# Six first products of the Mish layer inside the retention steps, two second products behind it, the first k in PSUM banks of its own, the second group of q a step sooner

## The chip, the core and the metric

The kernel runs on one core of one Trainium2 chip. The metric is the device time of one execution in microseconds (us). The engines named below are PE (TensorE), DVE (VectorE), ACT (ScalarE), POOL (GpSimd) and SP (SyncE, which here only issues transfers). Each engine takes its own instructions strictly in the order in which they stand in the program.

## What is computed

```python
# q, k, v: (4, 8, 576, 64); x: (2304, 512) tokens
scores = (q @ k^T) / sqrt(64)
ret = scores * Dmat              # Dmat[h] = gamma_h ** (i - j) for i >= j, else 0
x = (ret @ v)                    # (4, 8, 576, 64) -> (2304, 512)
h = x @ w_in                     # (2304, 512) @ (512, 2048)
x = (h * tanh(softplus(h))) @ w_out          # Mish; (2048, 512)
g = x @ w_gate; val = x @ w_val              # (512, 1536) each
out = (silu(g) * val) @ w_out2               # (1536, 512)
```

All in float32. PE multiplies each wide product as three products of two-part operands (a rounded part and the rest of it), so every weight and every activation is first split into such a pair.

## The kernel before

**Retention.** 20 steps `t`: 4 batches, each in 4 chunks of 128 positions and a last one of 64. In a step PE computes the scores of the chunk (`s`, line 505), transposes the next chunk's k and a part of a later q (`turn`, line 436, out to `kT` and `qT` by ACT, a few by DVE), then the product with the running state (`o`, line 575), the new state (`state`, line 549) and the masked scores times v (`o`, line 585), for which DVE must have masked the scores (`p`, line 515). DVE then scales `o` into the tokens `x` (line 598). All transposes go through one PSUM tile with the tag `tt`, so a `turn` waits until the one before it has been copied out.

**Weights.** `w_in` and `w_out` come as 32 pieces of 512 KB, in the order of the list `todo`: in0 to in4, out0, in5, out1, and so on to in15, out11, and then out12 to out15. Counted from 0, in5 is piece 6 and out12 is piece 28. A piece is fetched into one of four buffers `raw`, and takes five instructions of DVE and ACT in two or three passes: ACT scales one half (line 114) and DVE shifts the other (line 115); DVE puts the sign in (line 119) and joins the halves (line 123); ACT casts the first part of the result (line 133), and DVE (in retention POOL) subtracts it to get the second (line 134, `u<-raw,u`). Only then is the piece ready for PE and its buffer is free for the piece four places later. In retention one such pass, with one fetch, stands at the end of each step that is not in `REST`.

**Slots.** The Mish layer runs on blocks of 384 tokens, the first two blocks as 32 slots `s` (16 of each block). The first product of a slot is `g1(s)` (`h`, line 682, 12 matmuls on piece in`s`), its Mish, cast and rest are made by ACT and DVE (lines 733, 740, 744), and the second product `g2(s)` (`acc`, line 716, 12 matmuls on piece out`s`) comes four slots later. `EARLY` is the list of retention steps that hold a first product each: between the transposes and the state products of that step. After retention, `slot(s)` writes `g1(s)`, `g2(s - 4)`, then the Mish of slot `s`, and behind it the passes over further weight pieces: as many as are needed until `2 * s` pieces are done, and then one or two more. `plain1(i)` sends three finished weight quarters back to memory, for the third and later blocks, which use a Strassen scheme (lines 904 and 1298). Everything behind the slots is the same program before and after.

The rows call the weight pieces' buffers `raw`, the finished pieces `u`, and the transposed q and k `qT` and `kT`.

Of the kernel before, what the change touches and what calls it, by code (L numbers as in the profile page):

```python
# [7 lines left out]
F32 = mybir.dt.float32  # L8
# [9 lines left out]
def retention_mish_swiglu(  # L18
# [17 lines left out]
    nc = tc.nc  # L36
    B, H, S, D = q.shape
    NT, DM = out.shape
    F1 = w1_in.shape[1] // 128
    F2 = w2_gate.shape[1] // 128  # L40
    KT = DM // 128
    NP = H // 2
# [3 lines left out]
    LAG = 4  # L46
# [3 lines left out]
    W = (12, 3, 3)  # L50
    NC = 2
    RATES, AHEAD = (2.9, 3.3, 0.4, 1.28, 0.9, 1.0), 45
    EARLY = (9, 11, 14, 17)
    REST = (9, 14, 18, 19)

    xp = ctx.enter_context(tc.tile_pool(name="xp", bufs=1))
    cr = ExitStack()
# [325 lines left out]
    def retention(g1, mish, g_hi, g_lo):  # L383
        with ExitStack() as c0:
# [39 lines left out]

            def turn(name, *items):
                items = [x for x in items if x]
                if not items:
                    return  # L430
                p = ps1.tile([128, 2, 2, NP, 64], F32, tag="tt", name=f"t{name}")
                for z, (n, src, _) in enumerate(items):
                    for pr in range(NP):
                        for r in range(-(-n // 64)):
                            own = slice(64 * r, min(64 * r + 64, n))
                            nc.tensor.transpose(p[:, r, z, pr, :own.stop - own.start], src(pr)[own], ident[own, own])
                for z, (_, _, empty) in enumerate(items):
                    empty(p[:, :, z])

            def q_item(b, g, e, eng=nc.scalar.copy):  # L440
                if b >= B:
                    return None
                x = qkv["q", b, g]
                if g == nsc // 2:
                    n = S - 256 * g
                    qT[b, g] = at.tile([128, NP, n], F32, tag="qTl", name=f"qT{b}_{g}", bufs=1)
                    return (
                        n, lambda pr: x[:, 2 * pr:2 * pr + 2, :],
                        lambda p: nc.scalar.copy(out=qT[b, g], in_=p[:, 0, :, :n]),
                    )  # L450

                def empty(p):
                    if e == 0:
                        qT[b, g] = at.tile([128, NP, 256], F32, tag="qT", name=f"qT{b}_{g}")
                    for r in range(2):
                        (nc.vector.tensor_copy if (b, g, r) == (0, 1, 1) else eng)(
                            out=qT[b, g].rearrange("p a (h n r) -> p h a n r", r=2, h=2)[64 * e:64 * e + 64, :, :, :, r],
                            in_=p[64 * r:64 * r + 64],
                        )

                return 128, lambda pr: x[:, 2 * pr + e, :, :], empty

            def k_item(t):
                if t >= len(steps):
                    return None
                b, sc, n = steps[t]
                src = qkv["k", t]

                def empty(p):
                    kT[t] = at.tile([128, NP, 128], F32, tag="kT", name=f"kT{t}")  # L470
                    if n <= 64:
                        nc.scalar.copy(out=kT[t][:, :, :n], in_=p[:, 0, :, :n])
                    else:
                        nc.scalar.copy(out=kT[t].rearrange("p a (h n) -> p h a n", h=2), in_=p)

                return n, lambda pr: src[:, 2 * pr:2 * pr + 2, :], empty
# [5 lines left out]

            def q_next(t):
                b, sc, n = steps[t]
                due = (b, 1, sc) if sc < 2 else (b, 2, 0) if sc == 2 else (b + 1, 0, sc - 3)
                return q_item(*due) if b or sc > 1 else None

            def scale_v(t):
                if t >= len(steps):
# [42 lines left out]
            due = []  # L532
# [7 lines left out]
            def state(t):  # L540
                b, sc, n = steps[t]
                if sc == nsc - 1:
                    return
                if sc == 0:
                    stp[b] = ps1.tile([128, NP, D], F32, tag="st", name=f"state{b}")
                for pr in range(NP):
                    for e in range(2):
                        h = 2 * pr + e
                        nc.tensor.matmul(
                            stp[b][64 * e:64 * e + 64, pr, :],  # L550
                            lhsT=qkv["k", t][:n, h, :],
                            rhs=vs[t][:n, h, :],
                            start=(sc == 0 and pr == 0),
                            stop=(sc == nsc - 2),
                            skip_group_check=True,
                        )
# [11 lines left out]
            def output(t):  # L568
                b, sc, n = steps[t]
                o = ps1.tile([128, NP, 128], F32, tag="o", name=f"o{t}")  # L570
                if sc:
                    for pr in range(NP):
                        for e in range(2):
                            own = slice(64 * e, 64 * e + 64)
                            nc.tensor.matmul(  # L575
                                o[own, pr, :n], lhsT=sbd[:, pr, own], rhs=q_cols(t)[:, pr],
                                start=(pr == 0), stop=False, skip_group_check=True,
                            )
                state(t)
                if t == 1:  # L580
                    turn("q0_1", q_item(0, 1, 0), q_item(0, 1, 1))
                state_out(t)
                for pr in range(NP):
                    for e in range(2):
                        nc.tensor.matmul(  # L585
                            o[64 * e:64 * e + 64, pr, :n],
                            lhsT=vs[t][:n, 2 * pr + e, :],
                            rhs=pp[t][:n, e, pr, :n],
                            start=(sc == 0 and pr == 0), stop=True, skip_group_check=True,
                        )  # L590
                t0 = b * S + sc * 128
                done = 0
                while done < n:
                    j, off = divmod(t0 + done, T)
                    m = min(n - done, T - off)
                    if j not in xt:
                        new_x(xt, j, "x")
                    nc.vector.tensor_tensor(
                        out=xt[j][:, :, off:off + m],
                        in0=o[:, :, done:done + m],  # L600
                        in1=gout[:, :, sc * 128 + done:sc * 128 + done + m],
                        op=ALU.mult,
                    )
                    done += m
                    if j < 2 and off + m == T:
                        due.extend((j, kk) for kk in range(KT if j == 0 else XS - KT))
# [25 lines left out]
            warm(W[0])  # L632
            turn("q0_0", q_item(0, 0, 0), q_item(0, 0, 1, nc.vector.tensor_copy))
            warm(W[1])
            turn("k0", k_item(0))
            scale_v(0)
            warm(W[2])
            for t in range(len(steps)):
# [36 lines left out]
    with tc.manual_schedule():  # L675
# [70 lines left out]
        def slot(s):  # L746
            b, i = divmod(s, F1)
            if i == 0 and s:
                g2(s - LAG)
            g1(s)  # L750
            if s >= LAG and i:
                g2(s - LAG)
            d, nm, j = xt, "x", b + 1
            parts = () if b + 1 == NC else (i - F1 + 4,) if b and F1 - 4 <= i < F1 - 2 else range(2, KT) if i == F1 - 1 else ()
            mish(s)
            for kk in parts:
                split_hi(d, nm, j, kk)
            g_hi(s)
            g_lo(s)
            for kk in parts:  # L760
                split_lo(d, nm, j, kk, nc.vector)
            if s < F1 + OFF:
                while stage[3] < min(2 * s, n1):
                    run(weights(n1))
            if s >= LAG:
                g2_out(s - LAG)
            if s < F1 + OFF and not parts:
                for _ in range(1 + s % 2):
                    run(weights(n1, True))
            if s == len(EARLY):  # L770
                plain1(0)
            if s % 2 and s > len(EARLY) and s // 2 - 1 < F1 // 2:
                plain1(s // 2 - 1)
            if stage[3] >= n1:
                (third if third.ahead else second)(RATES[s >= F1 + OFF])
            if s == F1 + OFF:
                second(0.0)
# [293 lines left out]
                    second(RATES[3])  # L1071

        FIN1 = (6, 8, 8, 8, 6, 6, 6)
        for s in range(len(EARLY), NS):
            slot(s)
            if s == NS - F1 + 2:
                ya, yb = ysteps("e0", xt[NC], xt[NC + 1])
                ahead += ya + yb[0] + yb[1]
            if s > NS - F1 + 2:
                pop(ahead, 1 + s % 2)  # L1080
            if s >= NS - F1 + 10:
                stream1(s - (NS - F1 + 10))
# [329 lines left out]
```

## Time and profile before

| | |
|---|---|
| median of 3 runs | 892.86 us (890.14 to 893.03) |
| the profiled execution | 894.11 us, of which 892.3 us between its first and its last instruction |
| PE busy in that span | 871.9 us (98%) |
| DVE busy | 652.9 us (73%) |
| ACT busy | 426.6 us (48%) |
| POOL busy | 53.1 us (6%) |

The span is the stretch that the trace covers; times in the rows below are counted from its start. Retention takes it up to 106.4 us, the slots from there to about 225 us. Busy shares are means over stages with different limits, and they don't say which engine another one waits for.

### The profile page before, as it was taken

What the parts mean: (1) busy time and instruction counts of PE and PEld (TensorE: products, weight loads), DVE (VectorE), ACT (ScalarE), POOL (GpSimd) and SP (SyncE); (2) the same over time, 40 slices, a digit from 0 to 9 for tenths busy, and PEclk for the clock granted to TensorE, in tenths of its full rate; (3) what the DMA queues carried; (4) which work ended last, traced back from release to release, by engine and by line L of the source; (5) the groups of instructions that cost most, each with busy time, mean ns of one, the idle gap of its engine ahead of it and who ended that gap; (6) DMA issues with size and microseconds to landing.
All of it is one profiled execution on the core that took longest, in us unless ns stands there. A gap on an engine that the chain in (4) does not pass through costs nothing.

```text
span 892.3 us, 16688 instructions
## 1 busy us (share of the span) xinstructions
PE 871.9 (98%) x6330; PEld 842.0 (94%) x6330; DVE 652.9 (73%) x1271; ACT 426.6 (48%) x835; POOL 53.1 (6%) x47
## 2 busy tenths in 40 slices
PE   7888999999999999999999999999999999999998
PEld 7777899999999999999999999999999999999998
DVE  3886788998777786777786878876676776575772
ACT  3776566645656556565664424263212263222260
POOL 3654300000000000000000000000000000000000
PEclk9999999999999999999999999999999999999999
DMA  9999578577899985799978698978877878877773
GB/s 210 253 231 250 155 209 263 177 236 252 303 325 315 338 285 165 235 335 342 320 269 280 214 335 310 306 245 274 295 251 244 250 252 270 291 256 252 251 246 119
DMA packets 161600, 232.21 MB, mean 260 GB/s; under 512 B 48240, under 2 KB 124272, under 8 KB 161520
## 3 DMA queue, kind: packets, MB, share of 16 engines
q1 hardware_dynamic: 159984, 229.94, 81.4%
q10 hardware_dynamic: 1536, 1.21, 0.5%
q8 instruction: 50, 0.82, 0.4%
q14 instruction: 30, 0.25, 0.1%
HBM read 178.68 MB, written 52.43 MB: 259 GB/s over the span
## 4 chain that ended last, share of the span: by engine, by line
PE 85%; DVE 5%; DMA 5%; ACT 3%; issue 1%; POOL 1%; SPq 0%; ACTq 0%; POOLq 0%; DVEq 0%
PE t L904 29%; PE T L1298 15%; PE te L904 12%; PE e0a L975 7%; PE e1a L975 6%; PE h L682 5%; PE acc L716 4%; DMA raw<-in_moe_w_out_dram 3%; PE s L505 1%; DMA raw<-in_moe_w_in_dram 1%; PE o L585 1%; PE acc L950 1%; DMA v<-in_v_dram 1%; PE idle L630 1%; PE o L575 1%
## 5 line engine op out<-in xcount | busy, mean ns | idle before, releaser
L904 PE MATMUL t<-y,su 128*128 128x384 f32 x1512 | 267.6, 337 | 0.7 <-DVE u L911 0.4
L904 PEld LDWEIGHTS t<-y,su 128*128 128x128 f32 x1512 | 263.8, 188 | 2.9 <-DVE u L911 0.7
L904 PE MATMUL te<-ye,eu 128*128 128x384 f32 x672 | 136.1, 337 | 0.5 <-DVE scratch L911 0.5
L1298 PE MATMUL T<-su,g 128*128 128x256 f32 x1134 | 135.7, 282 | 0.0
L1298 PEld LDWEIGHTS T<-su,g 128*128 128x128 f32 x1134 | 135.6, 190 | 0.0
L904 PEld LDWEIGHTS te<-ye,eu 128*128 128x128 f32 x672 | 113.5, 188 | 5.0 <-DVE scratch L911 0.7
L975 PE MATMUL e1a<-ge,u 128*128 128x512 f32 (+1 forms) x384 | 76.2, 337 | 0.0
L975 PE MATMUL e0a<-ge,u 128*128 128x512 f32 (+1 forms) x384 | 76.1, 337 | 0.0
L682 PE MATMUL h<-xs,u 128*128 128x384 f32 x384 | 72.2, 337 | 0.0
L975 PEld LDWEIGHTS e1a<-ge,u 128*128 128x128 f32 x384 | 61.9, 188 | 6.0
L975 PEld LDWEIGHTS e0a<-ge,u 128*128 128x128 f32 x384 | 62.0, 188 | 5.8
L682 PEld LDWEIGHTS h<-xs,u 128*128 128x128 f32 x384 | 66.8, 188 | 0.3
L716 PE MATMUL acc<-g,u 128*128 128x384 f32 x336 | 63.4, 337 | 1.5 <-DVE u L134 0.9
L716 PEld LDWEIGHTS acc<-g,u 128*128 128x128 f32 x336 | 58.6, 188 | 2.4 <-DVE u L134 1.5
L1167 ACT ACTIVATE sg<-sg 128x384 f32<-128x384 f32 x54 | 28.4, 525 | 58.5 <-DVE sg L911 58.5
L1196 ACT COPY p<-t 128x384 f32<-128x384 f32 x35 | 16.5, 473 | 80.7 <-PE t L904 80.7
L1130 ACT CAST g<-ga 128x384 fp32r<-128x384 f32 x72 | 32.5, 514 | 43.2 <-DVE ga L1175 32.4
L911 DVE TENSOR_TENSOR u<-t,p 128x384 f32<-128x384 f32 x36 | 20.1, 557 | 40.3 <-PE t L904 40.2
L914 DVE TENSOR_TENSOR g<-ga,g 128x384 fp32r<-128x384 f32 x72 | 36.2, 553 | 6.4 <-ACT g L1130 6.2
L911 DVE TENSOR_TENSOR scratch<-te,scratch 128x384 f32<-128x384 f32 x48 | 26.7, 555 | 13.0 <-PE te L904 10.3
L911 DVE TENSOR_TENSOR v<-t,p 128x384 f32<-128x384 f32 x36 | 20.1, 557 | 17.0 <-PE t L904 16.9
L114 ACT ACTIVATE raw<-raw 128x512 f32<-128x512 f32 x32 | 22.1, 692 | 17.7 <-DMA raw<-in_moe_w_out_dram 12.5
(169 smaller groups left out, 1199.5 us busy)
## 6 DMA issues: line engine op xcount, KB each, us to landing
su<-comb SPq DMA_DIRECT2D x126, 512.0 KB, 4.3
su<-fcomb SPq DMA_DIRECT2D x63, 512.0 KB, 4.2
eu<-ecomb SPq DMA_DIRECT2D x56, 512.0 KB, 5.5
comb<-c SPq DMA_DIRECT2D x48, 256.0 KB, 4.8
raw<-in_moe_w_in_dram SPq DMA_DIRECT2D x16, 512.0 KB, 5.8
raw<-in_moe_w_out_dram SPq DMA_DIRECT2D x16, 512.0 KB, 5.4
ecomb<-e SPq DMA_DIRECT2D x32, 256.0 KB, 2.8
ecomb<-u SPq DMA_DIRECT2D x24, 256.0 KB, 4.6
```

The lines of the kernel that those rows point to most:

```text
L114: nc.scalar.activation(hi.bitcast(F32), hi.bitcast(F32), AF.Copy, scale=2.0 ** -112)
L505: nc.tensor.matmul(s[:n, e, pr, :n], lhsT=kT[t][64 * e:64 * e + 64, pr, :n], rhs=q_cols(t)[64 * e:64 * e + 64, pr], start=True, stop=True,)
L682: nc.tensor.matmul(ps, lhsT=u[:, a, kk * 128:(kk + 1) * 128], rhs=s[:, e, :], start=(c == 0), stop=(c == n - 1),)
L716: nc.tensor.matmul(accs[b][d][:, :T], lhsT=u[:, a, d * 128:(d + 1) * 128], rhs=g[:, e, :], start=(i == 0 and c == 0), stop=(i == F1 - 1 an ...
L904: nc.tensor.matmul(p, lhsT=w[:, (high, 1 - high)[a], kk * 128:(kk + 1) * 128], rhs=y[kk][:, x, :], start=begin and kk == 0 and (a, x) == ( ...
L911: nc.vector.tensor_tensor(out=out_, in0=a, in1=b_, op=ALU.add)
L914: nc.vector.tensor_tensor(out=out_, in0=a, in1=b_, op=ALU.subtract)
L975: nc.tensor.matmul(o, lhsT=u[:, a, d * 128:(d + 1) * 128], rhs=y[:, :512] if r == 0 else y[:, 512:], start=f == 0 and (a, x) == (0, 0) and ...
L1130: nc.scalar.copy(out=gt[n, c, i][:, 0], in_=x)
L1167: nc.scalar.activation(x, bank_ if part_ is None else x, AF.Silu)
L1196: (nc.scalar.copy if n or i or z else nc.vector.tensor_copy)(out=r["p1"], in_=p)
L1298: nc.tensor.matmul(p[m], lhsT=g[:, x, m * 128:(m + 1) * 128], rhs=w[:, 1 - a, :], start=begin and i == 0 and (a, x) == (0, 0) and not (sha ...
```

## The change

The numbers of `EARLY` and `REST` change: six first products in steps 8, 10, 12, 14, 16 and 18 in place of four in 9, 11, 14 and 17, and five steps without a pass over weights in place of four. Two second products, `g2(0)` and `g2(1)`, then stand by themselves between retention and the first slot, which is slot 6. The first three slots hold two more passes each, and `plain1` comes a pair of slots later. At the start, the first k is transposed into the banks of `o` and `st` and copied out by ACT and DVE, a half each; the second group of q is transposed in two halves, one with the k of step 1, and one ahead of that step's state.

```diff
-    EARLY = (9, 11, 14, 17)
-    REST = (9, 14, 18, 19)
+    EARLY = (8, 10, 12, 14, 16, 18)
+    REST = (9, 13, 17, 18, 19)
...
+            def first_k():
+                n, src, _ = k_item(0)
+                p = [ps1.tile([128, NP, 64], F32, tag=tag, name=f"tk0_{tag}") for tag in ("o", "st")]
+                halves(n, src, lambda r, pr: p[r][:, pr])
+                kT[0] = at.tile([128, NP, 128], F32, tag="kT", name="kT0")
+                for r, copy in enumerate((nc.scalar.copy, nc.vector.tensor_copy)):
+                    copy(out=kT[0][:, :, 64 * r:64 * r + 64], in_=p[r])
...
-                due = (b, 1, sc) if sc < 2 else (b, 2, 0) if sc == 2 else (b + 1, 0, sc - 3)
-                return q_item(*due) if b or sc > 1 else None
+                due = (b, 1, sc if b else 0) if sc < 2 else (b, 2, 0) if sc == 2 else (b + 1, 0, sc - 3)
+                return q_item(*due) if b or sc else None
...
+                if t == 1:
+                    turn("q0_1", q_item(0, 1, 1))
                 state(t)
-                if t == 1:
-                    turn("q0_1", q_item(0, 1, 0), q_item(0, 1, 1))
...
-            turn("k0", k_item(0))
+            first_k()
...
-                for _ in range(1 + s % 2):
+                for _ in range(2 if s < len(EARLY) + 3 else 1 + s % 2):
                     run(weights(n1, True))
...
-            if s % 2 and s > len(EARLY) and s // 2 - 1 < F1 // 2:
-                plain1(s // 2 - 1)
+            if s % 2 and s > len(EARLY) and s // 2 - 2 < F1 // 2:
+                plain1(s // 2 - 2)
...
+        for s in range(len(EARLY) - LAG):
+            g2(s)
         for s in range(len(EARLY), NS):
             slot(s)
```

PE's rows around the end of retention, before: the last step's three groups (`s`, `o`, `o`), then slot 4 with its first product `h` and the second product `acc` of slot 0.

```order
L505 MATMUL s_1684<-qT_2_1559,kT_1645 64x64 x8
L575 MATMUL o_1696<-qT_2_1559,sbd 64x64 x8
L585 MATMUL o_1696<-p_1693,vs_1647 64x64 x8
L682 MATMUL h_1731<-xs_0_544,u_889 128x384 x3
...
L716 MATMUL acc_0_1744<-g_1072,u_981 128x384 x2
```

The same place of the changed program, from step 18's transposes on.

```order
L431 MATMUL t_1658<-ident,k_1486 128x64 x4
L694 MATMUL h_1667<-xs_0_546,u_1133 128x384 x3
...
L587 MATMUL o_1680<-qT_1_1447,sbd 64x128 x8
...
L517 MATMUL s_1708<-qT_2_1591,kT_1663 64x64 x8
L587 MATMUL o_1720<-qT_2_1591,sbd 64x64 x8
L597 MATMUL o_1720<-p_1717,vs_1665 64x64 x8
L728 MATMUL acc_0_1759<-g_1006,u_983 128x384 x2
```

A first product has moved into step 18, and behind the last step stands a second product, with no first product ahead of it.

DVE's rows from the end of retention on, before: the last `x`, then the rest of slot 4's Mish (`g`), one pass over a weight piece (lines 119, 115, 123), slot 5's `g`, and two passes.

```order
L598 TENSOR_TENSOR x_1538<-o_1696,gout 128x4x64
L744 TENSOR_TENSOR g_1762<-m_1760,g_1762 128x384
L119 SCALAR_TENSOR_TENSOR raw_1469<-raw_1469 128x512
L115 TENSOR_SCALAR raw_1545<-raw_1545 128x512
L123 SCALAR_TENSOR_TENSOR raw_1469<-raw_1469 128x512
L744 TENSOR_TENSOR g_1762<-m_1799,g_1762 128x384
L119 SCALAR_TENSOR_TENSOR raw_1545<-raw_1545 128x512
L134 TENSOR_TENSOR u_1804<-raw_1469,u_1804 128x512
L115 TENSOR_SCALAR raw_1626<-raw_1626 128x512
```

DVE's rows at the same place of the changed program: the last `x`, the `g` of slot 5 (whose product is in step 18), the `g` of slot 6, and then two passes before the `g` of slot 7.

```order
L610 TENSOR_TENSOR x_1570<-o_1720,gout 128x4x64
L756 TENSOR_TENSOR g_1643<-m_1738,g_1643 128x384
L756 TENSOR_TENSOR g_1814<-m_1812,g_1814 128x384
L119 SCALAR_TENSOR_TENSOR raw_1414<-raw_1414 128x512
L115 TENSOR_SCALAR raw_1488<-raw_1488 128x512
L123 SCALAR_TENSOR_TENSOR raw_1414<-raw_1414 128x512
L119 SCALAR_TENSOR_TENSOR raw_1488<-raw_1488 128x512
L134 TENSOR_TENSOR u_1824<-raw_1414,u_1824 128x512
L115 TENSOR_SCALAR raw_1577<-raw_1577 128x512
L123 SCALAR_TENSOR_TENSOR raw_1488<-raw_1488 128x512
L756 TENSOR_TENSOR g_1814<-m_1860,g_1814 128x384
```

The passes over pieces now begin behind the `g` of slot 6, and the first of them is over piece 12, where it was piece 13.

## Rows read from the trace of the kernel before

**Rows 1.** Busy times by stretch: length, PE, weight loads, DVE, ACT, POOL, clock, DMA, GB/s

```profile
2.00:91.00 89.00, 78.12 (x1295) 69.63 (x1295) 59.57 (x89) 55.14 (x107) 46.53 (x38) 0.98 1.08 241
75.00:80.00 5.00, 2.81 (x41) 2.34 (x38) 2.76 (x6) 4.87 (x10) 2.39 (x2) 0.79 0.99 248
```

**Rows 2.** PE's longest wait from 20 to 106 us: total, times, longest

```profile
PE o L585 <- DVE p L515: 8.1, 9, 2.2
```

**Rows 3.** Waits from 106 to 162 us, PE's and DVE's longest

```profile
PE acc L716 <- DVE u L134: 0.9, 2, 0.6
...
DVE g L744 <- ACT g L740: 8.0, 7, 2.9
```

**Rows 4.** PE's longest wait after 162 us

```profile
PE te L904 <- DVE scratch L911: 0.5, 1, 0.5
```

**Rows 5.** ACT in time: start, us, operation; idle before it, and until what

```profile
34.35 0.68 ACT L114 ACTIVATE raw<-raw 128x512 f32<-128x512 f32 x1 [1.43 <-DMA raw<-in_moe_w_in_dram]
...
74.83 0.74 ACT L114 ACTIVATE raw<-raw 128x512 f32<-128x512 f32 x1 [3.10 <-DMA raw<-in_moe_w_out_dram]
```

**Rows 6.** PE in time, ahead of the first step

```profile
10.28 0.47 PE L436 MATMUL tk<-ident,k 64*128 64x64 f32 x8 [2.10 <-DVE qT L456]
```

**Rows 7.** PE in time: first rows of steps 9 to 12, 18, 19; slot 4

```profile
53.37 0.68 PE L505 MATMUL s<-qT,kT 64*64 64x64 f32 x16
...
58.36 1.16 PE L505 MATMUL s<-qT,kT 64*128 64x128 f32 x16
...
61.50 1.16 PE L505 MATMUL s<-qT,kT 64*128 64x128 f32 x16
...
67.74 1.16 PE L505 MATMUL s<-qT,kT 64*128 64x128 f32 x16
...
77.88 1.97 PE L585 MATMUL o<-p,vs 128*64 128x128 f32 x16 [2.19 <-DVE p L515]
...
99.88 1.16 PE L505 MATMUL s<-qT,kT 64*128 64x128 f32 x16
...
103.86 0.68 PE L505 MATMUL s<-qT,kT 64*64 64x64 f32 x16
...
106.36 2.35 PE L682 MATMUL h<-xs,u 128*128 128x384 f32 x12
```

**Rows 8.** PE in time: `h` of slots 5, 6, 16 and `g2(12)`

```profile
110.62 2.24 PE L682 MATMUL h<-xs,u 128*128 128x384 f32 x12
...
114.78 2.24 PE L682 MATMUL h<-xs,u 128*128 128x384 f32 x12
...
158.79 2.19 PE L716 MATMUL acc<-g,u 128*128 128x384 f32 x11 [0.61 <-DVE u L134]
160.81 4.33 PE L682 MATMUL h<-xs,u 128*128 128x384 f32 x24
```

**Rows 9.** DVE in time: slot 4's `g`, and passes of slots 5, 7, 14

```profile
109.81 0.56 DVE L744 TENSOR_TENSOR g<-m,g 128x384 fp32r<-128x384 f32 x1 [2.91 <-ACT g L740]
...
115.05 0.69 DVE L134 TENSOR_TENSOR u<-raw,u 128x512 fp32r<-128x512 f32 x1
...
122.29 0.56 DVE L744 TENSOR_TENSOR g<-m,g 128x384 fp32r<-128x384 f32 x1 [0.62 <-ACT g L740]
122.77 0.69 DVE L119 SCALAR_TENSOR_TENSOR raw<-raw 128x512 uint32<-128x512 uint32 x1
...
123.97 0.42 DVE L115 TENSOR_SCALAR raw<-raw 128x512 uint32<-128x512 uint32 x1
124.31 0.69 DVE L123 SCALAR_TENSOR_TENSOR raw<-raw 128x512 uint32<-128x512 uint32 x1
...
126.69 0.69 DVE L123 SCALAR_TENSOR_TENSOR raw<-raw 128x512 uint32<-128x512 uint32 x1
...
158.05 0.69 DVE L134 TENSOR_TENSOR u<-raw,u 128x512 fp32r<-128x512 f32 x1
```

**Rows 10.** Fetches of raw pieces, issued from 115 to 153 us

```profile
DMA to landing us min/median/max: 3.5/4.9/5.8
```

More of the change, by code (lines that the diff above doesn't have):

```diff
@@ L423, in retention, with halves @@
             qT, kT, vs, pp = {}, {}, {}, {}
+            def halves(n, src, to):
+                for pr in range(NP):
+                    for r in range(-(-n // 64)):
+                        own = slice(64 * r, min(64 * r + 64, n))
+                        nc.tensor.transpose(to(r, pr)[:, :own.stop - own.start], src(pr)[own], ident[own, own])
             def turn(name, *items):
@@ L432, in turn @@
                 for z, (n, src, _) in enumerate(items):
[L433 to L436, printed above, removed]
+                    halves(n, src, lambda r, pr: p[:, r, z, pr])
                 for z, (_, _, empty) in enumerate(items):
                     empty(p[:, :, z])
+            def first_k():
[5 more added lines that the diff above has]
+                    copy(out=kT[0][:, :, 64 * r:64 * r + 64], in_=p[r])
             def q_item(b, g, e, eng=nc.scalar.copy):
```

## The prediction, made before the changed kernel had run

> **What bounds the kernel now.** I read the busy times by stretch first, then the waits, then the engines in time. From 2 to 91 us the transfers are busy without a pause (DMA share 1.08 at 241 GB/s), while PE has work in 78.1 of 89 us [rows 1]. So for most of retention the stream of q, k, v and weight pieces sets the pace. It reaches PE by a detour: ACT and DVE come to a piece that has not landed and stand in front of it (1.43 us at 34.35, 3.10 at 74.83, and two such waits between, [rows 5]); the masked scores `p` are queued behind it on DVE, and PE waits for `p`, 8.1 us in nine waits [rows 2], the longest 2.19 us at 77.88 [rows 7].
>
> In the slots PE's longest waits are for weight pieces (0.9 us in two, [rows 3]), last for piece 28 (out12): DVE's rest of it starts at 158.05 and ends at 158.74 [rows 9], and the second product that needs it goes on at 158.79 [rows 8]. So the passes over weights end last there, with little to spare. In the same stretch DVE itself waits 8.0 us for ACT's `g` [rows 3]: it has room, because PE comes to each slot late. After 162 us the longest wait of PE is 0.5 us [rows 4], so what is gained or lost at 160.81, where slot 16's first product starts [rows 8], reaches the end nearly whole.
>
> **First k and second q.** They take away the 2.10 us in which PE waits for `tt` to be copied out [rows 6] and a smaller wait in step 2; new is a copy of half of k on DVE, behind its q copies. I cost both at nothing: what covers them is the fetch at 34.35, for which ACT already waits 1.43 us [rows 5]. Coming there sooner makes that wait longer, since the stream in front has the same bytes and no pause. Without that cover the gain would be at most the 2.10 us, and it would still have to pass the later landings.
>
> **Six products within retention.** Up to step 12 the changed kernel holds three first products where there were two, and the landing at 74.83 stays where it is. Step 12 began at 67.74 with two products done; now again two are done (steps 8 and 10), so I start there. Lengths of steps come from the starts in rows 7: an ordinary step with a product 6.24 (61.50 to 67.74), without 3.98 (99.88 to 103.86), a first chunk 3.14 (58.36 to 61.50), a short chunk with a product 4.99 (53.37 to 58.36), the last step 2.50 (103.86 to 106.36). With products in 12, 14, 16 and 18: 67.74 + 6.24 + 3.98 + 4.99 + 3.14 + 6.24 + 3.98 + 6.24 + 2.50 = 105.05, against 106.36 now. So two products more end 1.3 us sooner: they fill the waits before `p`. Included is that PE keeps full speed: from 75 to 80 us it worked 2.81 of 5 us and had a granted clock of 0.79 [rows 1], and one `o` took 1.97 us [rows 7]; with work in that gap I take the full clock (2.4 GHz). T is the end of retention from here on. If the clock drops again, or the products push other work back, the 1.3 us are lost and T = 106.4; I allow about as much to the other side, T = 104.0, since the steps taken as patterns hold short waits of their own.
>
> **Two second products ahead of slot 6.** Two products take 4.16 us (110.62 to 114.78, [rows 8]). Slot 6's `h` starts at 105.05 + 4.16 = 109.2 in place of 114.78: PE is 5.6 us ahead.
>
> **The passes over weights.** Here the gain has to survive. 13 pieces were done in retention, now 12, since one more step is in `REST`. And the passes begin later in the program: behind the `g` of slot 6, not of slot 4. A `g` starts 3.45 us after its `h` (109.81 against 106.36, [rows 7, 9]), so at 112.65; DVE stands idle for some 7 us ahead of it, and all passes are queued behind that instruction. After `g` 0.48, one pass without a rest 1.54, a sign 0.60 and a rest 0.69 piece 12 is ready at 116.0. Before, piece 13 was ready at 115.74 [rows 9]. So DVE has 16 pieces in front of it up to piece 28, where it had 15, from the same instant.
>
> How fast can they go? Before they took (158.74 − 115.74) / 15 = 2.87 us each, but with room. Two bounds. First DVE alone: two passes and a `g` took 5.00 (122.29 to the second join's 126.69 + 0.60, [rows 9]), 2.50 each. Second the four buffers: a fetch leaves when the piece four places before is done, takes 3.5, 4.9 in the middle, or 5.8 us [rows 10], then come shift 0.34, join 0.60, a full pass 2.14 (1.54 + 0.60), sign and rest 1.20, and two `g` of 0.48: 5.24. With 4.9 this is 10.1 / 4 = 2.54, with 5.8 it is 11.0 / 4 = 2.76. (Issuing takes the path too, but from SP's queue, where only the sends of `plain1` stand; these come a pair of slots later now.) Between 2.50 and 2.76 I take the middle, 2.63, because groups of three passes in slots 7, 11 and 13 make the landings uneven. Piece 28: 116.0 + 16 × 2.63 = 158.1, against 158.74. The two passes more in slots 6 and 8 don't change the sum: DVE is never without work there.
>
> So the sum is −0.6 us at piece 28, and as much at the end: 894.11 − 0.6 = 893.5 for the profiled execution, which lies 1.25 above the median. Against the median of 892.86 I predict **892.3**. PE alone would reach slot 16's `h` after ten first and eleven second products, 109.2 + 21 × 2.08 = 152.9; it gets there near 160, and the difference stands as waits for `u` in slots 11 to 16. So the 5.6 us are given back.
>
> The Trainium skill ("DMA: Bandwidth & Descriptors", section "Anatomy of one DMA — SWDGE (gpsimd) path") fits a transfer as about 2 us plus its bytes over 436 GB/s, for transfers issued from GpSimd. An estimate from that page for 512 KB is 3.2 us. The rows have that only as their shortest (3.5) and 4.9 in the middle [rows 10], with other transfers under way, so the measurement decides. By the page's figure the buffers would allow 2.1 us a piece and DVE's 2.50 would bind.
>
> **Rivals.** 0.3% (2.7 us) is about what a measurement of this kernel can tell from no change.
> - *The passes keep up* (faster). At DVE's own 2.50 piece 28 is ready at 156.0, and with T = 104.0 at 154.9: 2.7 to 3.8 us sooner, 889.0 to 890.1. For it: half of the landings are quicker than 4.9, and DVE's 8.0 us of waits for `g` go away. Against: at the middle landing the buffers are no faster than 2.54, and ACT's casts come in between. That the page's rule on transfer times holds here is this rival. Chance 0.28.
> - *The fetches slow the passes* (slower): sixteen pieces and the sends of `plain1` go out closer together, a landing takes longer, and each piece waits for it. It decides from (158.74 + 2.7 − 116.0) / 16 = 2.84 us a piece, that is a landing of 4 × 2.84 − 5.24 = 6.1 us, just above the 5.8 seen. At 2.90, piece 28 is at 162.4: +3.7, 896.5. With T = 106.4 it decides from 2.76 already. For it: in retention the same transfers, under a full stream, made ACT wait 3.10 us [rows 5]. Chance 0.15.
> - *Retention does not end sooner*: the products push `p` and the copies back as much as they fill, T = 106.4, piece 28 at 159.4, +0.7, 893.6. It has the likeliest one's sign of no change, chance 0.10.
>
> **How the numbers follow.** No measurable change is the likeliest, 0.47 for the sum as it stands and 0.10 for a retention that ends no sooner: 0.57. Its own range goes from 890.2 to 895.5 (0.3% to both sides). The range that should hold the time takes in the bounds of T and of the pace: 154.9 at the quick end (−3.8), and at the slow end T = 106.4 with 2.76 a piece, 117.4 + 44.2 = 161.6 (+2.8): 889.0 to 895.7. Faster 0.28, same 0.57, slower 0.15.
>
> **What would show it.** Right: the wait of 2.19 us and most of the 8.1 us for `p` are gone, the clock near 77 us is full; ACT's first waits for raw pieces are longer than before by what the start gained; retention ends between 104 and 106 us; DVE has no wait for `g` from slot 7 on; PE's waits for `u` in the slots grow from 0.9 to some 5 us or more; slot 16's `h` starts at 158 to 162. Wrong: if slot 16's `h` starts before 158, the pieces came faster than DVE's 2.50 or earlier than 116.0; if the waits for `p` stay, retention is not filled; if something after 162 us waits for DVE, the gain is lost there.

## The result, and the profile of the changed kernel

The changed kernel takes **896.96 us** (median of 6 runs, 895.51 to 897.58), beside 892.7 us (890.14 to 893.12) for the kernel before in the same comparison: a ratio of 1.0051, 95% interval 1.0037 to 1.0065. It is slower by half a per cent, and outside the range of 889.0 to 895.7. Its profiled execution took 897.34 us with a span of 895.5, against 894.11 and 892.3.

Retention did what was forecast. Busy times by stretch of the changed kernel, with the columns of [rows 1]:

```profile
2.00:91.00 89.00, 81.10 (x1298) 72.24 (x1298) 64.69 (x94) 57.68 (x112) 45.97 (x38) 0.98 1.09 245
75.00:80.00 5.00, 5.00 (x102) 4.57 (x99) 3.35 (x6) 4.08 (x9) 2.37 (x3) 1.00 0.99 251
```

From 75 to 80 us PE is now busy throughout, with a granted clock of 1.00 instead of 0.79. The waits up to 105 us have one line for the masked scores (total us, times, longest), where [rows 2] had 8.1 us in nine; the 2.19 us at 77.88 are gone, and a wait of 2.30 us has come up at 57.48, in step 9, which held a product before:

```profile
PE o L597 <- DVE p L527: 4.4, 5, 2.3
```

PE in time (start, us, operation; idle before it, and until what) from the end of retention:

```profile
105.41 4.43 PE L728 MATMUL acc<-g,u 128*128 128x384 f32 x24
109.67 2.24 PE L694 MATMUL h<-xs,u 128*128 128x384 f32 x12
...
142.13 0.44 PE L728 MATMUL acc<-g,u 128*128 128x384 f32 x1 [2.06 <-ACT u L133]
...
150.32 0.62 PE L694 MATMUL h<-xs,u 128*128 128x384 f32 x2 [1.12 <-ACT u L133]
151.56 3.43 PE L694 MATMUL h<-xs,u 128*128 128x384 f32 x10 [0.62 <-DVE u L134]
...
162.02 2.20 PE L728 MATMUL acc<-g,u 128*128 128x384 f32 x11 [0.39 <-DVE u L134]
164.06 4.33 PE L694 MATMUL h<-xs,u 128*128 128x384 f32 x24
```

Retention ends at 105.41 (forecast 105.05; before 106.36, [rows 7]), the two second products fill the next 4.3 us, and slot 6's `h` starts at 109.67 (forecast 109.2), 5.1 us ahead of 114.78 in [rows 8]. But slot 16's `h` starts at 164.06, where [rows 8] has 160.81: 3.25 us **later**. The whole loss stands there, since the span grew by 3.2.

DVE in time shows how. Slot 6's `g`, the rest (line 134) of piece 12, and that of piece 28, which answers to the last line of [rows 9]:

```profile
113.02 0.56 DVE L756 TENSOR_TENSOR g<-m,g 128x384 fp32r<-128x384 f32 x1 [6.61 <-ACT g L752]
...
115.88 0.69 DVE L134 TENSOR_TENSOR u<-raw,u 128x512 fp32r<-128x512 f32 x1 [0.16 <-ACT u L133]
...
161.28 0.68 DVE L134 TENSOR_TENSOR u<-raw,u 128x512 fp32r<-128x512 f32 x1
```

DVE stands for 6.61 us at slot 6's `g` with every pass behind it. Piece 12 is ready at 115.88 + 0.69 = 116.57 (forecast 116.0), piece 28 at 161.96 (forecast 158.1; before 158.74). So sixteen pieces took 45.39 us, **2.84 us each**, where the forecast had 2.63 and the kernel before 2.87. Beside the kernel before that is one piece more (2.84), begun 0.83 us later (116.57 for 115.74), and 15 pieces 0.03 quicker: 3.2 us. The waits from 104 to 165 us say who stood where (total us, times, longest):

```profile
DVE g L756 <- ACT g L752: 8.5, 5, 6.6
...
ACT raw L114 <- DMA raw<-in_moe_w_out_dram: 5.6, 4, 2.0
...
ACT raw L114 <- DMA raw<-in_moe_w_in_dram: 3.6, 4, 1.8
...
DVE raw L115 <- DMA raw<-in_moe_w_out_dram: 2.4, 3, 1.2
PE acc L728 <- ACT u L133: 2.1, 1, 2.1
...
PE h L694 <- ACT u L133: 1.4, 2, 1.1
PE h L694 <- DVE u L134: 1.3, 2, 0.6
PE acc L728 <- DVE u L134: 1.1, 4, 0.4
```

PE's four lines make 5.9 us of waits for weight pieces, against 1.5 before; from the end of retention to slot 16's `h` PE took 58.65 us for 23 products that need 47.84 at 2.08 each, so it lost 10.8 in all (2.4 before: 54.45 for 25 products). ACT stood 9.2 us at pieces that had not landed. After 165 us PE's longest wait is 0.5 us, as in [rows 4].

### The profile page after: what moved, and what is told of

Its sections match the earlier page's. It is cut to its first block, busy times and chain, and to the rows that moved or that the text cites. A ratio compares the mean times of both kernels' runs of the same rounds, so it can differ in the third digit from the quotient of the medians.

```text
span 895.5 us, 16683 instructions
## 1 busy us (share of the span) xinstructions
PE 875.3 (98%) x6330; PEld 842.1 (94%) x6330; DVE 655.9 (73%) x1273; ACT 426.2 (48%) x835; POOL 50.9 (6%) x46
## 4 chain that ended last, share of the span: by engine, by line
PE 85%; DVE 7%; DMA 4%; ACT 2%; issue 1%; SPq 0%; DVEq 0%; ACTq 0%
PE t L916 29%; PE T L1312 15%; PE te L916 12%; PE e0a L987 7%; PE e1a L987 6%; PE h L694 5%; PE acc L728 4%; DMA raw<-in_moe_w_out_dram 3%; PE o L597 2%; PE s L517 1%; DVE raw L123 1%; PE o L587 1%; PE acc L962 1%; DVE raw L115 1%; DVE raw L119 1%
## 5 line engine op out<-in xcount | busy, mean ns | idle before, releaser
L694 PE MATMUL h<-xs,u 128*128 128x384 f32 x384 | 75.1, 344 | 2.8 <-ACT u L133 1.4
```

The costliest lines, as they stand in the source:

```text
L694: nc.tensor.matmul(ps, lhsT=u[:, a, kk * 128:(kk + 1) * 128], rhs=s[:, e, :], start=(c == 0), stop=(c == n - 1),)
```

## What could be the cause

- **Theory A**, the passes over weights: they begin only behind slot 6's `g`, one piece more is left for them, and a piece takes 2.84 us. All 3.2 us are lost there.
- **Theory B**, elsewhere: in the two edits of the front, or in what stands beside the passes in the slots.
- Within A it was open what sets 2.84 us: the round trip through the four raw buffers (A1), or what DVE and ACT have to do, the waits showing only where spare time falls (A2).

Eleven kernels were run, each timed against the kernel before. The first table gives the times; 0.1% is 0.9 us. The second is read from one profiled execution of each of them and of the kernel before: the end of retention, when the first piece left over from retention is ready (piece 13 where marked, else 12), when piece 28 is ready, the us a piece between these two, and the start of slot 16's `h`.

| kernel | median, us | ratio to before | 95% interval |
|---|---|---|---|
| changed kernel | 896.96 | 1.0051 | 1.0037 to 1.0065 |
| passes ahead of slot 6 | 889.13 | 0.9965 | 0.9954 to 0.9977 |
| 13 pieces in retention | 893.13 | 1.0016 | 1.0006 to 1.0026 |
| six raw buffers | 891.13 | 0.9994 | 0.9983 to 1.0006 |
| five raw buffers | 890.79 | 0.9997 | 0.9987 to 1.0008 |
| front undone | 898.05 | 1.0070 | 1.0053 to 1.0087 |
| slots' extra passes undone | 899.08 | 1.0083 | 1.0068 to 1.0098 |
| passes ahead, six buffers | 886.32 | 0.9941 | 0.9927 to 0.9955 |
| the same, 13 pieces | 886.52 | 0.9942 | 0.9927 to 0.9957 |
| passes ahead, six buffers, front undone | 887.49 | 0.9951 | 0.9938 to 0.9964 |
| before, six raw buffers | 889.50 | 0.9978 | 0.9968 to 0.9988 |
| before, front alone | 890.19 | 0.9990 | 0.9979 to 1.0001 |

| profiled execution of | retention ends | first piece | piece 28 | us a piece | `h` of slot 16 |
|---|---|---|---|---|---|
| before | 106.36 | 115.74 (13) | 158.74 | 2.87 | 160.81 |
| changed kernel | 105.41 | 116.57 | 161.96 | 2.84 | 164.06 |
| passes ahead of slot 6 | 105.31 | 109.29 | 154.47 | 2.82 | 156.55 |
| 13 pieces in retention | 105.00 | 116.14 (13) | 157.93 | 2.79 | 160.02 |
| six raw buffers | 104.04 | 115.18 | 155.04 | 2.49 | 157.12 |
| five raw buffers | 104.19 | 115.34 | 155.16 | 2.49 | 157.24 |
| front undone | 104.95 | 116.09 | 160.09 | 2.75 | 162.18 |
| slots' extra passes undone | 104.06 | 118.53 | 162.63 | 2.76 | 164.73 |
| passes ahead, six buffers | 104.27 | 108.26 | 148.79 | 2.53 | 152.25 |
| the same, 13 pieces | 106.42 | 110.41 (13) | 148.47 | 2.54 | 154.87 |
| passes ahead, six buffers, front undone | 106.55 | 110.54 | 151.07 | 2.53 | 154.53 |
| before, six raw buffers | 103.61 | 113.00 (13) | 153.64 | 2.71 | 155.78 |
| before, front alone | 102.09 | 111.46 (13) | 154.57 | 2.87 | 156.64 |

The end of retention scatters between executions: the six of the table whose retention is the changed kernel's end it anywhere from 104.04 to 105.41, and the two with the retention of before at 103.61 and 106.36; the whole table spans 102.09 to 106.55. So times of two profiles are compared from the end of retention on, and a microsecond between two kernels is taken from the timed runs.

## Experiments

**Three passes ahead of slot 6.** Two behind `g2(0)` and one behind `g2(1)`:

```diff
         for s in range(len(EARLY) - LAG):
             g2(s)
+            for _ in range(2 - s):
+                run(weights(n1, True))
```

> The changed kernel with three passes over weights put ahead of slot 6: two behind the first second product and one behind the next, so that DVE has them in front of slot 6's g. Theory A (the loss is that DVE stands 6.6 us at slot 6's g with all passes behind it, one piece more is left, and a piece takes 2.84 us): piece 12 is ready near 108.5 instead of 116.6, piece 28 near 153 to 156 instead of 162.0, slot 16's h starts at 155 to 158 instead of 164.1, and the time is 6 to 9 us below the changed kernel's 897.0, so 888 to 891. Rival B (the time is lost elsewhere: in the front, or to what stands in the slots beside the passes): slot 16's h starts at 163 or later and the time is 895 to 897. Rival C (the pace stretches to fill whatever room it gets, since PE's products set it): piece 28 comes sooner by less than half of the 8 us, time 893 to 895.

Measured 889.13 us, (1.0051 − 0.9965) × 892 = 7.7 us below the changed kernel. DVE in time:

```profile
108.60 0.69 DVE L134 TENSOR_TENSOR u<-raw,u 128x512 fp32r<-128x512 f32 x1
...
112.93 0.56 DVE L756 TENSOR_TENSOR g<-m,g 128x384 fp32r<-128x384 f32 x1 [0.33 <-ACT g L752]
```

Piece 12 is ready 7.3 us sooner, and slot 6's `g` is no later than before the edit (112.93 against 113.02), with 0.33 us of wait ahead of it in place of 6.61. The pace stays at 2.82, so all 7.5 us arrive at slot 16 (156.55). The late start alone is worth more than the whole loss. B and C fall.

**13 pieces in retention.** One step fewer without a pass:

```diff
-    REST = (9, 13, 17, 18, 19)
+    REST = (9, 13, 18, 19)
```

> The changed kernel with one step fewer without a pass in retention, so that 13 pieces are done there, as in the kernel before. Theory A: one piece of 2.84 us less in front of piece 28, which is ready near 159.1; the time falls by 2.5 to 3 us to 894.0 to 894.5, if retention still ends within 0.5 us of 105.4. Rival B (loss elsewhere): 896 to 898.

Measured 893.13 us, 0.35% or 3.1 us below the changed kernel: about one piece's 2.84 us, as A has it (2.5 to 3 us were expected).

**Six raw buffers in the slots.** The places of the last two pieces lend them until they are needed; two fetches go out at the first pass behind retention, and from then on one for each piece done:

```diff
-        if j >= min(lim, len(todo)) or j - stage[3] >= RAW:
+        if j >= min(lim, len(todo)) or j - stage[3] >= (6 if "b" in pools else RAW):
...
-        raw[j] = rp.tile([128, 2 * DM], U32, tag=f"raw{j % RAW}", name=f"raw{j}")
+        m = j % RAW if j < 16 else (4, 5, 0, 1, 2, 3)[(j - 16) % 6]
+        raw[j] = (rp if m < RAW else pools["b"]).tile([128, 2 * DM], U32, tag=f"raw{m}" if m < RAW else f"u{n1 - 6 + m}", name=f"raw{j}")
...
         fetch(lim + 3)
+        if "b" in pools:
+            fetch(lim + 3)
```

> The changed kernel with six buffers for raw pieces in the slots instead of four (two that the last pieces' places lend). Theory A1 (a piece's 2.84 us is the round trip through four buffers: fetch, shift, passes): ACT's and DVE's waits for raw pieces between 116 and 155 us (some 10 and 2.4 us) go away, a piece takes 2.5 to 2.6 us, piece 28 is ready at 157 to 158, and the time is 891.5 to 893. Rival A2 (the 2.84 us are what DVE and ACT need for a piece with the groups of three passes, the waits for raw are only where spare time shows): the waits for raw go, others take their place, a piece still takes 2.75 to 2.9, time 895.5 to 897.5. A third way: six fetches under way together slow each other, landing over 6 us, no gain.

Measured 891.13 us, 0.57% or 5.1 us below the changed kernel. All waits from 116 to 155 us in this kernel (its line 135 is the rest, line 134 the cast):

```profile
ACT u L134 <- DVE raw L124: 12.5, 13, 1.7
PEld acc L731 <- DVE u L135: 4.3, 4, 1.7
PE acc L731 <- DVE u L135: 3.1, 4, 1.4
PEld h L697 <- DVE u L135: 0.8, 2, 0.4
DVE u L135 <- ACT u L134: 0.2, 1, 0.2
```

No engine waits for a landing any more, nor DVE for `g`: a piece from piece 18 on lies landed for 3.6 to 5.6 us before its shift, where with four buffers ACT or DVE takes a piece up 0.2 us after it lands, as a mean over pieces 17 to 28. ACT now waits for DVE, and a piece takes 2.49 us: DVE's own pace (it is busy 9.7 of every 10 us from 115 to 155), which the forecast had at 2.50. A1 holds and A2 falls.

**Five raw buffers**, four and one lent in the same way; against the kernel with six:

```diff
-        if j >= min(lim, len(todo)) or j - stage[3] >= (6 if "b" in pools else RAW):
+        if j >= min(lim, len(todo)) or j - stage[3] >= (5 if "b" in pools else RAW):
...
-        m = j % RAW if j < 16 else (4, 5, 0, 1, 2, 3)[(j - 16) % 6]
+        m = j % RAW if j < 16 else (4, 0, 1, 2, 3)[(j - 16) % 5] if j < n1 - 1 else 0
```

> The changed kernel with five raw buffers in the slots (four, and one lent). Theory A1: the round trip of a buffer is 11.5 us (landing 4.9, the passes 6.6); through five buffers that is 2.3 us a piece, below DVE's own 2.5, so a fifth buffer alone does what six did: a piece takes 2.5 to 2.65 us, time within 1.5 us of the 891.1 that six gave. Rival: the gain of six came from two fetches that leave early, behind retention, more than from the trip: then half of the gain, 893.5 to 894.5.

Measured 890.79 us, again with 2.49 us a piece and no wait for a landing from 116 to 155 us: one more buffer is enough, and the rival's half of the gain falls.

**The front undone.** First k through the shared bank again, second group of q in its old place:

```diff
-            first_k()
+            turn("k0", k_item(0))
...
-                due = (b, 1, sc if b else 0) if sc < 2 else (b, 2, 0) if sc == 2 else (b + 1, 0, sc - 3)
-                return q_item(*due) if b or sc else None
+                due = (b, 1, sc) if sc < 2 else (b, 2, 0) if sc == 2 else (b + 1, 0, sc - 3)
+                return q_item(*due) if b or sc > 1 else None
...
-                if t == 1:
-                    turn("q0_1", q_item(0, 1, 1))
                 state(t)
+                if t == 1:
+                    turn("q0_1", q_item(0, 1, 0), q_item(0, 1, 1))
```

> The changed kernel with the two edits of the front undone (first k through the shared bank, second group of q in its old place). Theory A: the start up to step 2 is some 1 us later, the wait for the piece that lands near 34 us takes it up, retention ends at 105.4 plus or minus 0.4, and the time is within 1 us of the changed kernel's 897.0. Rival B (the front edits cost the loss): 892 to 894.

Measured 898.05 us, 0.19% above the changed kernel, with intervals that overlap. B's front falls, since undoing it should have been faster. But A's "within 1 us" missed too, by a size that this run can't tell from nothing, so the front was tried from two more sides: alone on the kernel before, and undone in the kernel where PE waits for no piece.

> The kernel before, with the two edits of the front alone (first k through banks of its own, second group of q sooner). As the prediction had it, the wait for the piece that lands near 34 us takes the gain up: within 1 us of before's 891.8. Rival: up to 2 us faster, because part of the front's gain passes the later landings.

> The kernel with three passes ahead of slot 6 and six raw buffers, with the two edits of the front undone. There PE waits for no piece, so each microsecond of retention's end reaches the end of the program. If the front edits are hidden: 886.3 plus or minus 0.7, and the 3.2 us that it has over the kernel before with six buffers (889.5) are the products' in the waits of retention. If they are not hidden: 887 to 888.5.

Measured 890.19 us (ratio 0.9990, the interval just reaches 1) and 887.49 us (0.9951 where 0.9941 stands with the front). The first lies on the border of its two expectations, the second where the front is not hidden. Three comparisons give 0.1, 0.1 and 0.2% in favour of the front edits. None is clear alone; together they speak for about 1 us, half of the 2.10 us in [rows 6]. The piece that was to take the gain up lands between 33.5 and 35.0 us in every profile, with the front and without. In the nine with the front ACT takes it up within 0.03 us, so it was waiting there; in two of the four without, ACT came 0.8 and 1.9 us after the landing, so that there nothing covered the later start. One execution of each kernel shows how a part can pass, not how much.

**The extra pass in slots 6 and 8 undone.**

```diff
-                for _ in range(2 if s < len(EARLY) + 3 else 1 + s % 2):
+                for _ in range(1 + s % 2):
```

> The changed kernel without the extra pass in slots 6 and 8 (1 + s % 2 passes everywhere, as in the kernel before). Theory A1 (the pace is the round trip through the buffers, so where the passes stand among the slots counts little): within 1 us of the changed kernel (here some 896.3). Rival A2 (groups of three passes bunch the releases and make the landings late): pieces at 2.7 us or less, 1.5 to 3 us less, 893 to 895. A third way: a piece's pass comes a slot later than it is needed, and it is slower by 1 to 3 us.

Measured 899.08 us, 0.32% or 2.9 us **above** the changed kernel: the third way. A1's "within 1 us" missed as well as A2. DVE in time:

```profile
111.67 0.56 DVE L756 TENSOR_TENSOR g<-m,g 128x384 fp32r<-128x384 f32 x1 [6.61 <-ACT g L752]
...
115.83 0.56 DVE L756 TENSOR_TENSOR g<-m,g 128x384 fp32r<-128x384 f32 x1 [2.06 <-ACT g L752]
...
117.85 1.51 DVE L134 TENSOR_TENSOR u<-raw,u 128x512 fp32r<-128x512 f32 x2
```

With one pass behind slot 6's `g`, the rest of piece 12, which belongs to the next pass, stands behind slot 7's `g`. Piece 12 is ready 118.53 − 108.33 = 10.2 us after the start of slot 6's `h`, and 116.57 − 109.67 = 6.9 us with the extra pass.

**The kernel before with six raw buffers.** The same edit, with the first borrowed buffer at piece 17, because piece 16 is already fetched in retention there:

```diff
-        m = j % RAW if j < 16 else (4, 5, 0, 1, 2, 3)[(j - 16) % 6]
+        m = j % RAW if j < 17 else (4, 5, 1, 2, 3, 0)[(j - 17) % 6]
```

> The kernel before, with six raw buffers in the slots in place of four and nothing else changed. Theory A1 (the 2.87 us a piece of the kernel before were already the round trip through four buffers, not room that DVE had): a piece takes 2.55 to 2.65 us, piece 28 is ready 3 to 4.5 us sooner, PE then has its floor at 110.6 + 21 second and first products, so slot 16's h starts at 158 to 159.5 in place of 160.8, and the time falls by 1.3 to 2.5 us to 889.5 to 890.5. Rival A2 (before, DVE had room, the pace was PE's demand, as the prediction read it): pieces still 2.8 to 2.9 us apart and the time within 0.7 us of 891.8.

Measured 889.50 us, 0.22% or 2.0 us below before. All waits from 116 to 155 us (line 747 is `g`, line 736 its Mish):

```profile
ACT u L134 <- DVE raw L124: 8.5, 10, 1.7
ACT m L736 <- PE h L685: 3.6, 4, 0.9
DVE g L747 <- ACT g L743: 2.9, 5, 0.7
```

The waits for landings and PE's waits for pieces are gone. From the end of retention to slot 16's `h` PE takes 52.17 us instead of 54.45. A piece takes 2.71 us, more than expected, because PE is now the bound (12 first and 13 second products at 2.08 are 52.0) and DVE waits for its `g`. That DVE waits for `g` tells the two kernels apart poorly: 2.9 us here, and 2.4 us in the same stretch with four buffers.

**Both remedies together**, and then 13 pieces in retention besides (there the first borrowed buffer is at piece 17 again):

> Both at once: three passes ahead of slot 6 and six raw buffers in the slots. Theory A (start of the passes and their pace are the two terms, and PE is the next bound): piece 12 near 108.6, pieces at 2.6 us each, piece 28 near 151, PE waits for no piece and is busy without a pause from 105 us on, slot 16's h starts at 153 to 155, some 2 us before the 156.6 of the kernel with the passes ahead alone; time 885.5 to 887.5 where that one has 889.1. Rival: with the transfers closer together the landings grow, h of slot 16 stays at 156.5 and the time at 889.

> Passes ahead, six buffers, and 13 pieces in retention instead of 12. Theory A with PE as the next bound: no piece is waited for already without the 13th in retention, so nothing is gained over the kernel with the first two; slot 16's h at 153 to 155, time 885.5 to 888. If pieces still bind there: another 2 us less.

Measured 886.32 and 886.52 us. Busy times of the first by stretch, and under them those of the changed kernel:

```profile
125.00:135.00 10.00, 10.00 (x59) 10.00 (x59) 9.71 (x20) 7.72 (x15) 0.00 (x0) 1.00 0.95 292
135.00:145.00 10.00, 10.00 (x60) 10.00 (x59) 9.87 (x20) 6.58 (x13) 0.00 (x0) 1.00 0.99 329
145.00:155.00 10.00, 10.00 (x59) 10.00 (x58) 8.92 (x17) 7.05 (x14) 0.00 (x0) 1.00 0.75 266
```

```profile
125.00:135.00 10.00, 8.83 (x46) 7.43 (x44) 9.06 (x17) 6.85 (x13) 0.00 (x0) 1.00 0.86 260
135.00:145.00 10.00, 7.38 (x38) 6.28 (x37) 8.61 (x17) 5.74 (x11) 0.00 (x0) 1.00 0.80 252
145.00:155.00 10.00, 8.25 (x38) 7.42 (x36) 8.01 (x15) 6.15 (x12) 0.00 (x0) 0.84 0.86 261
```

PE is busy throughout, and needs 152.25 − 104.27 = 47.98 us from the end of retention to slot 16's `h`: 2 + 21 products at 2.08 are 47.84. The rival's 889 falls, and a thirteenth piece in retention adds nothing. The first of the two is the fastest kernel of the study, 5.3 us (0.59%) below the kernel before, and 0.37% or 3.3 us below the kernel before with six buffers. In both of these PE waits for no piece, so the 3.3 us are what six products in retention and the front bring once the pieces keep up; without the front it is 0.9978 − 0.9951, some 2.4 us.

## Why the prediction was wrong

**The step that failed is the pace in "The passes over weights"**: a piece takes 2.84 us, not 2.63. Sixteen times 0.21 is 3.3 us, and the start was 0.57 late (116.57 for 116.0): together the 3.9 us by which piece 28 missed 158.1. Its two bounds, 2.50 and 2.76, did not hold the value.

*The trip through the buffers was mis-sized.* The forecast had 4.9 for the landing and 5.24 for what DVE does, 10.1 in all. In the changed kernel the trip from one release of a buffer to the next, as a mean over pieces 17 (ready at 130.36) to 28 (161.96), is 11.57 us: 0.03 to the issue, 4.92 to the landing, and 6.62 behind it. The landing was right, and SP's queue is not in the way. Behind the landing stand 0.82 until the shift begins, 0.54 until both halves are done, 1.02 until the sign, 2.31 from sign to joined, and 1.93 from joined to ready. The forecast's 5.24 for this counted only DVE's own operations, as if each found its place free. (A quarter of the trip is the pace again, as in any ring that is kept full: with six buffers the same measure gives 14.94 us, and 2.49 a piece. So the trip says where the time goes; that the ring binds is shown by the runs with five and six buffers.) One trip can be followed in the rows, that of piece 23: the release of its buffer by the rest of piece 19 on DVE, then its shift, sign, join and rest:

```profile
134.68 0.69 DVE L134 TENSOR_TENSOR u<-raw,u 128x512 fp32r<-128x512 f32 x1
...
140.84 0.43 DVE L115 TENSOR_SCALAR raw<-raw 128x512 uint32<-128x512 uint32 x1 [0.58 <-DMA raw<-in_moe_w_out_dram]
...
142.11 1.29 DVE L134 TENSOR_TENSOR u<-raw,u 128x512 fp32r<-128x512 f32 x2 [0.23 <-ACT u L133]
143.32 0.69 DVE L119 SCALAR_TENSOR_TENSOR raw<-raw 128x512 uint32<-128x512 uint32 x1
...
144.74 0.69 DVE L123 SCALAR_TENSOR_TENSOR raw<-raw 128x512 uint32<-128x512 uint32 x1
...
146.17 0.69 DVE L134 TENSOR_TENSOR u<-raw,u 128x512 fp32r<-128x512 f32 x1
```

Its fetch on SP's queue:

```profile
135.40 0.34 SPq L102 DMA_DIRECT2D raw<-in_moe_w_out_dram  x1
```

And ACT, with the half of piece 23 that it scales, and behind it the casts of pieces 21 and 22:

```profile
140.84 0.70 ACT L114 ACTIVATE raw<-raw 128x512 f32<-128x512 f32 x1 [1.77 <-DMA raw<-in_moe_w_out_dram]
141.43 1.21 ACT L133 CAST u<-raw 128x512 fp32r<-128x512 f32 x2
```

Released at 135.37, fetched at 135.40, landed when the shift could start at 140.84, but signed only at 143.32: two rests stand between, and those waited for ACT's casts, which had stood behind the same landing. It was ready at 146.86, 11.49 us after its buffer came free.

*"But with room" was the misreading.* The forecast took the 2.87 us a piece of the kernel before for demand, because DVE waited 8.0 us for `g` [rows 3]. The view of [rows 3] has more lines, which the forecast did not weigh:

```profile
ACT raw L114 <- DMA raw<-in_moe_w_out_dram: 6.0, 6, 1.8
ACT raw L114 <- DMA raw<-in_moe_w_in_dram: 2.3, 3, 1.5
...
PE acc L716 <- ACT u L133: 0.6, 1, 0.6
```

ACT stood 8.3 us at landings, and of pieces 17 to 28 ACT or DVE took nine up within 0.05 us of their landing (eight in the changed kernel, none with six buffers). The trip through its buffers, over the same pieces, is 11.62 us, with 4.95 for the landing and 6.62 behind it, the same as in the changed kernel; and with six buffers that kernel became 2.0 us faster. So the ring held it back too; 2.91 of the 8.0 us are one wait at slot 4's `g`, with all passes still queued behind it [rows 9]. Had 2.87 been carried over, the sum would have been 116.0 + 16 × 2.87 = 161.9, beside the measured 161.96; that it fits so closely would have been luck, since the start was 0.57 us late and the sixteen pieces together 0.5 us quicker.

**Point by point.**
- *Retention:* right in its place and near in size: the 2.19 us wait is gone from its place, the clock is full, and T was 105.41 for 105.05; of the 8.1 us for `p` not most but 3.7 are gone, and the longest is now 2.30 us in step 9. That T fell by 1.3 us can't be confirmed from single executions, given the scatter.
- *PE 5 us ahead, all of it given back as waits for `u`:* right; some 5 us were forecast and 5.9 came in PE's own rows, 10.8 by the whole stretch.
- *Late start:* right in place and size (6.61 us of DVE at `g`); its price, 7.7 us, was not in the sum, because it was set off against the same instant of the kernel before.
- *Front at nothing:* about 1 us too little, as far as three unclear comparisons tell. Its sign came: the first scores start 1.74 us sooner (10.02 for 11.76), and ACT's first two waits for pieces to land are 1.97 us at 24.82 and 1.26 at 29.21, where before it found the first piece landed and waited 0.19 for the second.
- *"The two passes more in slots 6 and 8 don't change the sum":* wrong. Without them the time is 2.9 us longer.
- *DVE without a wait for `g` from slot 7 on:* wrong; 8.5 − 6.6 = 1.9 us in four waits remain, since ACT stands at landings.
- *The end:* right. In every profile of the first table the stretch from slot 16's `h` to the last instruction is 730.9 to 731.5 us.
- *Rivals:* "The fetches slow the passes" had the right sign, and its point of decision, 2.84 us a piece, is what was measured; but its mechanism, landings of 6.1 us, did not happen (mean 4.92, before 4.95). "The passes keep up" at 2.50 came about only with a fifth buffer.
- *The Trainium skill's rule for a transfer:* by the estimate of 3.2 us for a landing (the Trainium skill, "DMA: Bandwidth & Descriptors", section "Anatomy of one DMA — SWDGE (gpsimd) path") the trip would be 3.2 + 6.65 = 9.9 us, 2.46 a piece, and the buffers would not bind. The rows have 4.9, and they do bind.

## What to carry to other kernels

Where a ring of buffers feeds an engine, the time from one release of a buffer to its next, divided by the number of buffers, is the pace whenever the ring is kept full, so it doesn't say by itself who binds. Two other things did here: whether a landed buffer is taken up at once (0.2 us after the landing with four buffers, 3.4 with six), and whether one buffer more changes the pace (from 2.84 to 2.49 us). A forecast of the trip has to hold the waits between the operations, and not the operations alone. An engine's idle time is room only if what it needs has landed. Work that is moved ahead on one engine pays only if what feeds it is moved ahead too, in front of the instruction that waits for that work: that order was worth 7.7 us here, a fifth buffer some 5, and the order with six buffers 9.8, from the changed kernel's 1.0051 to 0.9941.

## What was not expected of the hardware

A lower clock followed PE's waits. In the changed kernel PE was busy 8.83 and 7.38 of 10 us in the two stretches from 125 to 145 us; from 145 to 155 its granted clock was 0.84, a part of it at the lower of its two levels (1.2 GHz), and ten matmuls of `h` took 3.43 us at 151.56, where ten took 2.00 at 128.05. With six buffers PE was busy 9.54 and 8.57 in the same stretches and the clock stayed at 1.00. It is not seen to cost anything at the end here, since PE still waited 0.39 us for piece 28, before 162.02.

More fetches under way did not keep the pieces from coming faster. The medians from issue to landing for `w_out` and `w_in` pieces from 115 to 153 us are 4.4 and 5.0 us in the changed kernel and 5.0 and 4.9 in the kernel before, both with four buffers, 4.9 and 5.5 with six, 5.3 and 5.7 with six and the passes ahead. Each is of 3 to 9 landings, with other transfers beside them, so that the number of fetches makes them later is likely, and not shown.
